# Channel weights loaded by SyncE at the start in fp32, and a table's reordering moved behind two loads, in a sparse-attention and spectral-mixing kernel

## The chip, the cores and the metric

The kernel runs on one core of a Trainium2 chip. The metric is the device time of one execution in microseconds, the median of several runs; lower is better. The profile is one execution recorded by the hardware profiler on that core.

## The reference, cut to what matters

The first half is attention over 8 batches, 8 heads, 576 positions and 64 dimensions a head. Heads 0 to 3 see the last 32 positions ("local"), heads 4 to 7 see every 32nd position ("strided"). The second half takes the result as `x` (8 x 576 x 512), mixes its lowest 64 Fourier modes with two complex weight matrices per mode, and ends with a layer whose matrix is `w_ch`, the channel weights that the change is about.

```python
scores = np.where(masks[None, :, :, :], scale * q @ k.T, -1e9)   # local or strided mask by head
x = softmax(scores) @ v                                          # (8, 576, 512)
X = np.fft.rfft(x, axis=1)
Yr = np.einsum('bmd,mde->bme', Xr, w_r) - np.einsum('bmd,mde->bme', Xi, w_i)
Yi = np.einsum('bmd,mde->bme', Xr, w_i) + np.einsum('bmd,mde->bme', Xi, w_r)
y = np.fft.irfft(Y, n=S, axis=1)
u = x + y
return u + np.maximum(u @ w_ch, 0.0)                             # w_ch is 512 x 512
```

All inputs and the output are fp32 in DRAM. `w_r` and `w_i` are 64 x 512 x 512 each, 134 MB together, and are by far the largest input.

## The kernel before, in words

The kernel computes in f16 with fp32 sums. Loads from DRAM that GpSimd issues convert fp32 to f16 on the way; loads that SyncE (`nc.sync`) or ScalarE (`nc.scalar`) issue copy without converting. Each engine works through its own queue in the order in which the program emits instructions, and the order is written by hand.

The work comes in these stages:

1. **Strided heads**, a loop over 8 batches (L832). `load_str` (L214) brings v, q and k of one or two batches into a ring of 12 slots. `str_front` gives the steps that transpose them; `str_scores` and `str_values` compute attention into `xb`; `dft(b - 1, 1)` transforms the batch before with a table `cFs`. `load_loc` and `w_fetch`, at the head of each turn of the loop, issue later loads on GpSimd: q, k, v of the local heads and the first spectral weights.
2. **Local heads**, a second loop over 8 batches (L863), with `mode_pair` (L589), the spectral product for two modes, between the steps. In this loop's turn 6 stands the load of the channel weights, `w_ch_fetch` (L197).
3. **The other half of the modes**, with `w_turn` (L896), which reorders the channel weights on TensorE, and `premix` (L726), which multiplies x by them.
4. **The last modes and the output**, stored by SyncE (L1071).

The spectral weights are streamed through a ring of five pairs, `wring`. Three more pairs are guests: their place in memory belongs to a tile that is needed only later. The names of these places are in `GUEST = {1: "Y0", 2: "X0", 7: "YT"}` (L148), so pair 7 lies where the spectra tile `YT` comes later. `w_fetch` issues the next pair when a pair of places is free; `mode_pair` calls it after the products that freed one.

The Fourier table `cT` is loaded by SyncE. `strided_tokens` (L330), on GpSimd, clears two margins and writes a reordered copy of `cT` into the tile `PL`. `fourier(1)` (L338) transposes that copy on TensorE into the table `cFs`, which `dft(b, 1)` reads first in batch 1; `fourier(0)` makes the other table after batch 1. At the start GpSimd's queue holds, in this order: the loads of batches 0 and 1 (9 DMAs), `strided_tokens`, the loads of batches 2 and 3 (6 DMAs), and the first spectral weights. `fourier(1)` is emitted after the eighth of batch 0's ten front steps (L829).

Of the kernel before, what the change touches and what calls it, by code (L numbers as in the profile page):

```python
# [10 lines left out]
FP = mybir.dt.float32  # L11
# [7 lines left out]
DM = 512  # L19
# [37 lines left out]
def kernel(  # L57
# [10 lines left out]
    nc = tc.nc  # L68
# [3 lines left out]
    big = ctx.enter_context(tc.tile_pool(name="big", bufs=1))  # L72
# [13 lines left out]
    def psum(kind, half=False, pair=False):  # L86
        if pair:
            return pss[kind].tile([128, 2, 512], FP, tag=kind, name=kind)
        if half:
            return pss[kind].tile([128, 1024], F16, tag=kind, name=kind)  # L90
        return pss[kind].tile([128, 512], FP, tag=kind, name=kind)
# [15 lines left out]
    def const_load(eng, *which):  # L107
        for n in which:
            eng.dma_start(cs[n][:, 0 : hosts[names.index(n)].shape[1]], drams[n])
# [46 lines left out]
    w_chs = {}  # L156
    w_ch = big.tile([128, 4, DM], F16, name="w_ch")
# [3 lines left out]
    def w_fetch(n=1):  # L161
        free_pairs[0] += n
        while len(w_tiles) < 2 * NM:
            i = len(w_tiles)
            pair = i // 2
            nm = 4 if pair in QUADS else 2
            if 2 * free_pairs[0] < nm:
                return
            free_pairs[0] -= nm // 2
            half, m = ORDER[i]  # L170
            if pair in GUEST:
                wt = big.tile([128, 2, 4, DM], F16, tag=GUEST[pair], name="wt")
            else:
                a = 2 * ((pair - sum(g < pair for g in GUEST)) % NWBUF)
                wt = wring[:, a : a + nm]
            single = []
            for ri, src in enumerate((moe_w_r, moe_w_i)):
                dst = wt[ds(64 * ri, 64)].rearrange("p m c e -> p m (c e)")
                rows = src[m : m + nm, ds(256 * half, 256), :].rearrange(
                    "m (p c) e -> p m (c e)", c=4  # L180
                )
                if ri and not m:
                    dst, rows = dst[:, 1:nm], rows[:, 1:nm]
                if i in UNEVEN and not ri:
                    a = 0
                    for n in UNEVEN[i]:
                        nc.gpsimd.dma_start(dst[a : a + n], rows[a : a + n])
                        a += n
                elif i < 2 * NM - 4:
                    nc.gpsimd.dma_start(dst, rows)  # L190
                else:
                    single += [(j, ri, dst[:, j], rows[:, j]) for j in range(nm)]
            for _, _, to, rows in sorted(single, key=lambda x: x[:2]):
                nc.gpsimd.dma_start(to, rows)
            w_tiles.extend(wt[:, j] for j in range(nm))

    def w_ch_fetch():  # L197
        nc.gpsimd.dma_start(w_ch, moe_w_ch.rearrange("(c p) e -> p c e", p=128))
        w_chs["n"] = w_ch

# [11 lines left out]
    def load_str(b, nb):  # L214
        for vi in (2, 0, 1):
            n = 3 * (b % 4) + SLOT[vi]
            two = ring[:, n : n + 4 : 3, :]
            src = SRC[vi][b - b % 2 : b - b % 2 + 2, 4:8].rearrange(
                "b h (c r) d -> (h c) b (r d)", r=32
            )  # L220
            if nb == 2:
                nc.gpsimd.dma_start(two[0:64], src[0:64])
            else:
                nc.gpsimd.dma_start(ring[0:64, n, :], src[0:64, b % 2])
            if b % 2 == 0:
                nc.gpsimd.dma_start(two[64:72], src[64:72])

    def load_loc(*bs):
        for b in bs:
            if b >= B:  # L230
                return
            for vi in (2, 0, 1):
                nc.gpsimd.dma_start(
                    loc_in(b, vi),
                    SRC[vi][b, 0:4].rearrange("h (cb i) d -> (h cb) (i d)", i=18),
                )
# [17 lines left out]
    def act_copy(out, in_):  # L254
        nc.scalar.activation(out=out, in_=in_, func=ACTF.Copy)  # L255
# [74 lines left out]
    def strided_tokens():  # L330
        nc.gpsimd.memset(cs["cT"][:, S:640], 0.0)
        nc.gpsimd.memset(PL[:, S : S + NCB], 0.0)
        nc.gpsimd.tensor_copy(
            out=PL[:, 0:S].rearrange("p (q r c) -> p q r c", q=2, c=NCB),
            in_=cs["cT"][:, 0:S].rearrange("p (c r q) -> p q r c", q=2, r=16),
        )

    def fourier(half):  # L338
        tp = psum("tp", half=True)
        n, nt = (108, 6) if half else (128, 5)  # L340
        for t in range(nt):
            if half:
                lhs = PL[:, ds(288 * (t // 3) + NCB * JG[t % 3][0], 108)]
            else:
                lhs = cs["cT"][:, ds(128 * t, 128)]
            nc.tensor.transpose(tp[0:n, ds(128 * t, 128)], lhs, idn)
        F = cs["cFs"] if half else cs["cFl"]
        src = tp[0:n, 0 : 128 * nt].rearrange("p (t g r m) -> p r t g m", t=nt, g=4, r=2)
        for r in range(2):
            (nc.vector.tensor_copy if r else act_copy)(  # L350
                out=F[0:n, 1 + r].rearrange("p t (g m) -> p t g m", g=4), in_=src[:, r]
            )
        nc.vector.tensor_scalar(
            out=F[0:n, 0], in0=F[0:n, 2], scalar1=-1.0, scalar2=None, op0=AluOp.mult
        )
# [433 lines left out]
    const_load(nc.scalar, "cI", "cM6", "cM5")  # L789
    load_str(1, 1)  # L790
    const_load(nc.sync, "cT", "cMl")
    strided_tokens()
    load_str(2, 2)
    w_fetch()

    def str_front(b):
        return [
            lambda: str_v(b, 0), lambda: str_v(b, 1),
            lambda: str_v(b, 2), lambda: str_q(b, 0),
            lambda: str_back(b, 0),  # L800
            lambda: str_back(b, 1), lambda: str_q(b, 1),
            lambda: str_k(b, 0),
            lambda: str_k(b, 1), lambda: str_k(b, 2),
        ]
# [13 lines left out]
    for i, w in enumerate(first):  # L818
        w()
        if i == 0:  # L820
            nc.vector.memset(vT[:, 1152:1216], 0.0)
            for t in v16:
                nc.vector.memset(t[:, :, 0:2], 1.0)
                nc.vector.memset(t[:, :, 130:132], 1.0)
        if i == 2:
            nc.vector.memset(PS, 0.0)
        if i == 5:
            nc.vector.memset(kzs[1], 0.0)
        if i == 7:  # L829
            fourier(1)  # L830
    SPLIT = [0, 2, 4, 5, 7, 8, 10]
    for b in range(B):  # L832
        if b in (1, 3):
            load_str(b + 3, 2)
        load_loc(*[(), (), (), (), (0,), (1, 2), (3,), (4, 5)][b])
        w_fetch([2, 1, 1, 1, 1, 1, 0, 0][b])
        front = str_front(b + 1) if b + 1 < B else loc_front(0)
        for t in range(6):
            str_scores(b, t)
            if b > 0:  # L840
                if t < 2:
                    str_values(b - 1, 4 + t)
                elif t == 2:
                    dft(b - 1, 1)
            if t >= 2:
                str_values(b, t - 2)
            for w in front[SPLIT[t] : SPLIT[t + 1]]:
                w()
        if b == 1:
            nc.vector.memset(PL[:, 0:PS0], 0.0)  # L850
            fourier(0)
# [11 lines left out]
    for b in range(B):  # L863
        load_loc(b + 6)
        front = loc_front(b + 1) if b else [lambda: None] * 4 + front1[4:]
        scores = [lambda h=h: loc_scores(b, h, False) for h in range(4)]
        ends = [lambda h=h: loc_scores(b, h, True) for h in (0, 2)]
        values = [lambda h=h: loc_values(b, h) for h in range(4)]
        work = [
            scores[0], front[0], scores[1], ends[0], front[1], values[0], front[2],  # L870
            scores[2], front[3], values[1], scores[3], front[4], ends[1], front[5],
            values[2], front[6], values[3], front[7], lambda: dft(b, 0),
        ]
        if b == 6:
            work.insert(0, w_ch_fetch)
        n = 0
        nm = NMODES[b]
        for mi in range(nm):
            upto = -(-len(work) * (mi + 1) // nm)
            for w in work[n:upto]:  # L880
                w()
            n = upto
            mode(0, sum(NMODES[:b]) + mi)
# [12 lines left out]
    def w_turn(half, cp):  # L896
# [14 lines left out]
    work = [  # L911
        lambda half=half, cp=cp: w_turn(half, cp) for half in range(2) for cp in range(2)
    ]
# [76 lines left out]
    for n, i in enumerate([3, 5, 7] + list(range(8, 21))):  # L990
        b, t = n // 2, n % 2 * 2
# [158 lines left out]
```

## Time and profile before

| | us |
|---|---|
| median of 3 runs | 426.48 |
| the three runs | 425.19, 426.83, 426.48 |
| span of the profiled execution, first to last instruction | 423.3 |
| TensorE busy in the span | 336.8 (80%) |
| VectorE, ScalarE, GpSimd busy | 234.9, 218.8, 95.3 |
| packets of GpSimd's DMA queue, share of 16 engines | 96.9% |

The profiled execution's own device time is not recorded apart from its span; the span lies 3.2 us below the median of the runs. In the profile PE is TensorE, DVE VectorE, ACT ScalarE, POOL GpSimd and SP SyncE; `L190` is line 190 of the kernel. The slices cut the span into 40 equal parts and give busy shares in tenths. DMA queue q0 is GpSimd's, q1 SyncE's, q10 ScalarE's. The bytes of a DMA are those that it writes, so an fp32 load that arrives as f16 reads twice as many. A weight load of one pair is two DMAs of 512 KB, one from `w_r` and one from `w_i`; some are four modes long, 1024 KB each.

### The profile page before, as it was taken

How to read it: one execution, taken by the hardware profiler on the slowest of the kernel's cores; microseconds unless marked ns; L12 is line 12 of the kernel's file. 1: busy time of each engine (PE TensorE's matmuls, PEld its weight loads, DVE VectorE, ACT ScalarE, POOL GpSimd, SP SyncE). 2: the span in 40 equal slices, each digit the busy share in tenths (PEclk: the TensorE clock that was granted, in tenths of full speed). 3: DMA queues.
4: the chain of work that ended last, by engine and by line, in shares of the span. 5: the costliest groups of instructions: out<-in, count | busy, mean ns of one | idle time of the engine just before them, and what ended most of it. 6: DMA issues, size and time to landing. Idle time of an engine off the chain costs nothing.

```text
span 423.3 us, 9718 instructions
## 1 busy us (share of the span) xinstructions
PE 336.8 (80%) x4164; PEld 204.2 (48%) x4164; DVE 234.9 (56%) x470; ACT 218.8 (52%) x391; POOL 95.3 (23%) x165
## 2 busy tenths in 40 slices
PE   2977878779999198889874959896778989888994
PEld 2866766654666055556542425453344534445331
DVE  3788878851455034545323325864385547555794
ACT  1687778642656056565753323622162356443772
POOL 7332333322422011102122102212101232210200
PEclk9999999957999689999998789999798999999999
DMA  8999999999999999999999999999999999998598
GB/s 147 213 213 213 214 211 214 210 212 211 214 213 213 215 213 216 213 215 214 212 215 212 213 213 214 214 213 214 213 213 210 210 212 216 212 214 163 198 379 316
DMA packets 30346, 91.62 MB, mean 216 GB/s; under 512 B 3872, under 2 KB 4640, under 8 KB 30304
## 3 DMA queue, kind: packets, MB, share of 16 engines
q0 software_dynamic: 24624, 81.28, 96.9%
q1 hardware_dynamic: 5248, 9.65, 6.2%
q8 instruction: 32, 0.52, 0.5%
q10 hardware_dynamic: 432, 0.08, 0.1%
q14 instruction: 10, 0.08, 0.0%
HBM read 162.83 MB, written 9.44 MB: 407 GB/s over the span
## 4 chain that ended last, share of the span: by engine, by line
PE 38%; DMA 36%; DVE 15%; ACT 5%; issue 3%; POOL 1%; DVEq 0%; POOLq 0%; ACTq 0%
DMA wring<-in_moe_w_i_dram 28%; PE y L601 9%; PE sc L739 5%; DMA ring<-in_q_dram 5%; DMA wring<-in_moe_w_r_dram 4%; DVE xb L245 3%; DVE yy L774 2%; ACT X L255 2%; DVE kz L287 2%; PE p L1010 2%; PE y L536 2%; PE tp L417 2%; PE sc L463 2%; PE sc L536 1%; PE p L1031 1%
## 5 line engine op out<-in xcount | busy, mean ns | idle before, releaser
L601 PE MATMUL y<-wring,X 128*32 128x512 f16 (+1 forms) x424 | 65.0, 418 | 25.8 <-DMA wring<-in_moe_w_i_dram 25.7
L190 POOL DMA_DIRECT2D wring<-in_moe_w_r_dram x39 | 23.5, 604 | 200.1 <-PE y L601 176.8
L601 PEld LDWEIGHTS <-X 128*32 128x32 f16 (+1 forms) x448 | 27.5, 139 | 43.4 <-DMA wring<-in_moe_w_i_dram 26.5
L749 DVE COPY xo<-tp 128x512 f16<-128x512 f16 x32 | 22.1, 692 | 36.9 <-PE tp L747 36.8
L748 ACT ACTIVATE v<-sc 128x512 f16<-128x512 f32 x32 | 19.1, 597 | 45.1 <-PE sc L739 45.1
L255 ACT ACTIVATE yr<-y 128x512 f16<-128x512 f32 x28 | 16.7, 597 | 43.2 <-PE y L601 43.0
L739 PE MATMUL sc<-w_cp,xT 128*128 128x512 f16 x128 | 36.1, 404 | 1.9 <-DVE xT L707 1.9
L245 DVE TENSOR_TENSOR xb<-av,rec 90x256 f16<-90x256 f32 (+2 forms) x80 | 36.0, 450 | 2.8
L493 ACT ACTIVATE PL<-sc 128x480 f16<-128x480 f32 (+1 forms) x48 | 26.9, 578 | 20.2 <-PE sc L479 19.9
L244 DVE RECIPROCAL rec<-av 90x4 f32<-90x4 f32 (+2 forms) x80 | 14.6, 183 | 37.8 <-PE av L508 28.3
L424 DVE COPY qT<-tp 128x576 f16<-128x576 f16 x16 | 11.9, 752 | 39.3 <-PE tp L417 39.3
L190 POOL DMA_DIRECT2D wring<-in_moe_w_i_dram x42 | 25.4, 605 | 9.8 <-DMA wring<-in_moe_w_i_dram 3.8
L984 DVE TENSOR_TENSOR xo<-p,xo 128x1024 f16<-128x1024 f32 x16 | 19.6, 1225 | 13.8 <-PE p L782 13.8
L382 ACT ACTIVATE PL<-sc 90x360 f16<-90x360 f32 (+1 forms) x48 | 22.7, 490 | 6.9 <-PE sc L375 6.4
L255 ACT ACTIVATE v<-p 128x1024 f16<-128x1024 f32 x16 | 16.4, 1023 | 17.1 <-PE p L782 17.1
L255 ACT ACTIVATE v<-tp 128x640 f16<-128x640 f16 (+1 forms) x24 | 19.0, 807 | 11.6 <-PE tp L451 8.8
L417 PE MATMUL tp<-cI_s,ring 64*64 64x64 f16 x864 | 22.8, 198 | 2.1 <-DVE qT L424 1.7
L463 PE MATMUL sc<-cMl_s,cI_s 128*128 128x480 f16 (+1 forms) x48 | 18.9, 393 | 5.2 <-ACT PL L493 3.6
L255 ACT ACTIVATE kz<-tp 64x360 f16<-64x360 f16 (+1 forms) x32 | 18.9, 592 | 6.2 <-PE tp L417 5.2
L280 PE MATMUL tp<-cI_s,ring 72*128 72x72 f16 x256 | 15.4, 207 | 8.4 <-DMA ring<-in_v_dram 6.9
L417 PEld LDWEIGHTS <-ring 64*64 64x64 f16 x864 | 18.0, 112 | 8.3 <-issue 4.2
L1054 ACT ACTIVATE rl<-p 128x1024 f32<-128x1024 f32 (+1 forms) x19 | 18.4, 979 | 4.9 <-PE p L1031 3.0
(146 smaller groups left out, 736.6 us busy)
## 6 DMA issues: line engine op xcount, KB each, us to landing
wring<-in_moe_w_r_dram POOLq DMA_DIRECT2D x17, 1024.0 KB, 13.5
wring<-in_moe_w_i_dram POOLq DMA_DIRECT2D x16, 1024.0 KB, 17.7
wring<-in_moe_w_i_dram POOLq DMA_DIRECT2D x24, 512.0 KB, 15.3
wring<-in_moe_w_r_dram POOLq DMA_DIRECT2D x22, 512.0 KB, 13.4
out_dram<-osb SPq DMA_DIRECT2D x14, 512.0 KB, 3.4
ring<-in_v_dram POOLq DMA_DIRECT2D x8, 288.0 KB, 13.3
ring<-in_q_dram POOLq DMA_DIRECT2D x8, 288.0 KB, 13.6
ring<-in_k_dram POOLq DMA_DIRECT2D x8, 288.0 KB, 13.1
```

The lines of the kernel that those rows point to most:

```text
L190: nc.gpsimd.dma_start(dst, rows)
L245: nc.vector.tensor_tensor(out=dst, in0=val.rearrange("p h (q c) -> p h c q", c=4), in1=rec[0:n, 0:pieces] .to_broadcast((n, pieces, 64)) . ...
L255: nc.scalar.activation(out=out, in_=in_, func=ACTF.Copy)
L382: nc.scalar.activation(out=PS[0:n, ds(POFF[t], 4 * n)], in_=scp[0:n, 0 : 4 * n], func=ACTF.Exp, scale=SCALE,)
L417: nc.tensor.transpose(tp[ds(64 * hp, 64), ds(64 * i, 64)], qn[ds(64 * hp, 64), ds(64 * (9 * g + i), 64)], idn[ds(64 * hp, 64), ds(64 * hp, ...
L463: nc.tensor.matmul(scp[:, 0 : n * times].rearrange("p (h x) -> p h x", h=times), idn, mask_rows("cMl", n, times), start=True, stop=False,)
L493: nc.scalar.activation(out=dst, in_=src, func=ACTF.Exp, scale=SCALE)
L601: nc.tensor.matmul(yp[ds(a, 32), :], Xh[half][pr, c].rearrange("p b r (h m) -> p (b r h) m", h=2)[:, :, mm % 32], wt[pr, XC[c], :], start= ...
L739: nc.tensor.matmul(vp, xT[:, ch], w_chs["cp"][:, ch, :], start=(ch == 0), stop=(ch == 3),)
L748: nc.scalar.activation(out=v0, in_=vp, func=ACTF.Copy)
L749: nc.vector.tensor_copy(out=xo.rearrange("p (h q c) -> p h q c", h=2, c=4), in_=tp[:, 0:512].rearrange("p (h c q) -> p h q c", h=2, c=4),)
L984: nc.vector.tensor_tensor(out=xo, in0=up[:, 0:n], in1=xo, op=AluOp.add)
```

## The change

The load of the channel weights moves from GpSimd's queue (turn 6 of the second loop) to SyncE's queue, behind the constants at the beginning. Since SyncE's loads do not convert, the weights arrive as fp32 in a tile of their own, `w_f`, that takes the place of `YT` and so of the guest weight pair 7. ScalarE then rounds a quarter of it to f16 into `w_ch` at the end of each of the batches 1 to 4 of the strided loop. On GpSimd, the loads of batches 2 and 3 go ahead of `strided_tokens`. `fourier(1)` moves from inside batch 0's front steps to the end of batch 0's turn.

```diff
-    def w_ch_fetch():
-        nc.gpsimd.dma_start(w_ch, moe_w_ch.rearrange("(c p) e -> p c e", p=128))
+    def w_ch_load():
+        w_chs["f"] = big.tile([128, 4, DM], FP, tag="YT", name="w_f")
+        nc.sync.dma_start(w_chs["f"], moe_w_ch.rearrange("(c p) e -> p c e", p=128))
         w_chs["n"] = w_ch
+
+    def w_ch_round(c):
+        act_copy(w_ch[:, c], w_chs["f"][:, c])
...
     const_load(nc.sync, "cT", "cMl")
+    w_ch_load()
+    load_str(2, 2)
     strided_tokens()
-    load_str(2, 2)
     w_fetch()
...
-        if i == 7:
-            fourier(1)
...
+        if b == 0:
+            fourier(1)
+        if 1 <= b <= 4:
+            w_ch_round(b - 1)
         if b == 1:
             nc.vector.memset(PL[:, 0:PS0], 0.0)
             fourier(0)
...
-        if b == 6:
-            work.insert(0, w_ch_fetch)
```

## The prediction

> **What bounds the kernel now.** I read the page's slices first, then the table of DMA queues.
>
> ```profile
> PE   2977878779999198889874959896778989888994
> DMA  8999999999999999999999999999999999998598
> GB/s 147 213 213 213 214 211 214 210 212 211 214 213 213 215 213 216 213 215 214 212 215 212 213 213 214 214 213 214 213 213 210 210 212 216 212 214 163 198 379 316
> q0 software_dynamic: 24624, 81.28, 96.9%
> ```
>
> From the second slice to about 389 us the DMA engines move 210 to 216 GB/s without a pause, nearly all of it in one queue: GpSimd's, which reads fp32 and writes f16. 81.28 MB at 212 GB/s are 383.4 us; with a start at about 3 us and the 1.5 us lost early (below) that makes 388 us, against the 390.6 us at which the last load is seen to land. TensorE has holes in the same slices. The chain of waits, in order of time, says who waits for whom:
>
> ```profile
> 110.63 15.19 DMA wring<-in_moe_w_r_dram
> 126.10 21.10 DMA wring<-in_moe_w_i_dram
> ...
> 346.62 14.75 DMA wring<-in_moe_w_i_dram
> 361.65 19.09 DMA wring<-in_moe_w_i_dram
> 381.03 9.58 DMA wring<-in_moe_w_i_dram
> 391.46 1.05 PE y L758 x4
> ```
>
> TensorE waits for weights again and again, and the last weights land at 390.61; what follows (32.7 us to the end of the span, 423.3) hangs on that landing. So the time is the stream's start, plus its bytes at 212 GB/s, plus what it loses where it runs below that, plus a fixed tail. An instruction on TensorE, ScalarE or GpSimd counts only if it starves the stream. The only place where it is visibly below rate is the beginning; the table of stretches shows that (columns: stretch, length, busy time of the five engines, TensorE clock, DMA share, GB/s):
>
> ```profile
> 1.50:3.00 1.50, 0.00 (x0) 0.00 (x0) 0.64 (x1) 0.90 (x1) 1.50 (x3) 1.00 0.81 183
> 3.00:4.50 1.50, 0.00 (x0) 0.00 (x0) 0.00 (x0) 0.38 (x1) 1.50 (x4) 1.00 0.90 120
> 4.50:6.00 1.50, 0.00 (x0) 0.00 (x0) 0.00 (x0) 0.00 (x0) 1.25 (x3) 1.00 1.08 176
> 6.00:7.50 1.50, 0.62 (x11) 0.65 (x12) 0.06 (x1) 0.00 (x0) 0.87 (x4) 1.00 1.06 161
> 7.50:9.00 1.50, 0.50 (x9) 0.32 (x6) 1.31 (x7) 0.83 (x2) 1.50 (x3) 1.00 1.00 191
> 9.00:10.50 1.50, 1.43 (x18) 1.46 (x19) 1.20 (x3) 0.00 (x0) 1.29 (x3) 1.00 1.05 199
> ...
> 207.00:214.00 7.00, 5.19 (x60) 3.27 (x57) 1.03 (x4) 4.31 (x9) 0.00 (x0) 1.00 1.12 210
> ```
>
> Against 213 GB/s the five stretches from 3.0 to 10.5 us lack 93, 37, 52, 22 and 14 GB/s, times 1.5 us: 327 KB, or 1.53 us of the stream. That is all the room that the beginning has. The last line is where the channel weights pass now: still 210 GB/s.
>
> **Part by part.** *The load taken out of GpSimd's queue.* 128 x 4 x 512 in f16 are 0.524 MB, and in 207:214 the stream kept its rate: 0.524 / 213 = 2.46 us. All that follows in the queue can come 2.46 us earlier. The issue itself (0.80 us on GpSimd at 197.28) lies before 7.46 us in which GpSimd waits for TensorE: nothing.
>
> *The load put on SyncE's queue.* It now writes fp32, 1.049 MB. No row shows an fp32 load, so I bound it. The stream reads two bytes for each one that it writes, 2 x 213 = 426 GB/s: 2.46 us. The fp32 output at the end (400:410) moves 380 GB/s: 2.76 us. I take 2.6: rows of 2 KB as in the output, but read from DRAM as in the stream. SyncE has the two constant loads ahead of it (0.74 to 1.56 us) and nothing behind it until the outputs at 394.96, so it is issued at about 1.6 and moves data from about 2.5 us, together with GpSimd's first loads. If the engines are full this takes 2.6 us away from GpSimd's queue, and the whole is +0.1. What it moves in the holes is free: at most the 1.53 us; at least the clear hole of 3.0:4.5, where the DMA share is 0.90 and 93 x 1.5 = 140 KB, 0.65 us, are missing. I take 1.2, nearer to the upper end, because GpSimd, not the engines, sets the early rate: it had issued eight DMAs when it had to sit 0.88 us for the first to land (below).
>
> The Trainium skill, page DMA: Bandwidth & Descriptors, section Issuing engines are not separate DMA queues, speaks against this change: DMAs from different issuing engines run on the same 16 engines and interleave, and only the issuing time is saved. By it the sum of the two loads is 2.46 out and 2.46 in, no change. The trace agrees with it wherever the engines are full, as in 207:214; the first 10 us are where they are not.
>
> *Loads of batches 2 and 3 ahead of the table's reordering.* GpSimd's timeline:
>
> ```profile
> 6.63 0.51 POOL L224 DMA_DIRECT2D ring<-in_k_dram  x1 [0.88 <-DMA ring<-in_v_dram]
> ...
> 7.26 1.17 POOL L333 COPY PL<-cT_s 128x576 f16<-128x576 f16 x1
> 8.37 0.59 POOL L222 DMA_DIRECT2D ring<-in_v_dram  x1
> ...
> 12.99 0.58 POOL L190 DMA_DIRECT2D wring<-in_moe_w_r_dram  x1 [0.70 <-DMA ring<-in_q_dram]
> ```
>
> The two memsets and the copy (7.13 to 8.43) leave the front of the six load issues and stand before the first weight issue. The first of the six can go 1.2 us earlier; the next ones wait for landings anyway, so the gain is between 0 and the 22 and 14 GB/s missing after 7.5 us (54 KB, 0.25 us), and that is already counted as room. The weights' first issue now stands behind 1.3 us of reordering, of which its own 0.70 us wait hides half. Seven DMAs (1.9 MB, 9 us) are in flight then, so the stream does not run dry; without that cover the cost would be 0.6 us. I take 0.
>
> *The table's transposes behind batch 0.* The same instructions, later: 6 transposes (0.80 us of TensorE), one ScalarE copy (0.49), two VectorE steps (0.36 + 0.26). Their first reader is the transform at 24.14, in batch 1. Batch 0 has 0.8 us less ahead of it. Nothing.
>
> *Four roundings on ScalarE.* The nearest row is the 128x512 fp32 to f16 copy at 597 ns, from PSUM: 4 x 0.60 = 2.4 us at the ends of batches 1 to 4 (about 31 to 60 us). Queued behind each are the next batch's exponentials, for which TensorE waits. So TensorE is up to 2.4 us later at 60 us, and up to 2.6 more because the first loads share the engines. It is covered: in 140:160 TensorE is busy 12.06 of 20 us, waiting for weights, and GpSimd's loads land 13 us after their issue, so the queue is that deep when its issues wait for TensorE (23.62, 26.52, 30.50). Uncovered it would be up to 5 us. The fp32 copy lies in the buffer of weight pair 7, whose load waits for the fourth rounding: about 60 us plus lateness, against an issue at 75.33. Nothing.
>
> **The sum.** -2.46 + 2.6 - 1.2 = -1.1 us; by the bounds from -1.5 (2.46 in, 1.53 in holes) to -0.35 (2.76 in, 0.65 in holes), and +0.3 with no hole. On the profiled execution: span 423.3 to 422.2. The median of the runs, 426.48, is 3.2 above this span; I carry that over: 425.4.
>
> **Rivals.** *Paid in full:* the holes are not idle engines but slow ones (the share reads 1.06 and 1.08 in 4.5:7.5, which speaks for it; the 0.90 before speaks against). Then -2.46 + 2.6 = +0.1: 426.6. This is also where the rule of the Trainium skill quoted above (DMA: Bandwidth & Descriptors) would put it.
>
> *Wholly hidden:* the channel weights fill 2.46 us of real idle time, with the head of the load before 3.0 us (share 0.81) counted in and the earlier issue filling the rest: 424.0. For it speaks that GpSimd's issue sets the early pace; against it, that only 1.53 us are missing from 3.0 on. A gain of more than 0.5% (2.13 us) needs this.
>
> *Turns cost more than bytes:* SyncE's rows alternate with GpSimd's packets on each engine, and each turn stalls the other queue. The trace has small packets of ScalarE's queue among GpSimd's, the last mask's, landing 5.4 us after issue where its twin took 2.5. If the whole loss of 1.53 us came from these masks (2 x 128 rows, 16 for each engine), a turn would cost 0.096 us, and 32 turns (512 rows of 2 KB over 16 engines) 3.1 us: -2.46 + 2.6 + 3.1 = +3.2, 429.7. It brings over 0.5% from 0.062 us a turn on. Against it: those masks have landed by about 7 us, and the loss goes on to 10.5.
>
> **How the numbers follow.** About 0.5%, 2.13 us, is what a measurement of this kernel can tell from no change (its three runs lie 1.64 us apart). Partly hidden, my forecast: 0.5. Paid in full: 0.18. Wholly hidden: 0.17. Turns, slower: 0.15. The first two fall within 0.5%, but runs scatter and the forecast's lower end is near the border, so I move 0.03 from them to faster: 0.20, 0.65 and 0.15. The range runs from wholly hidden, 424.0, past the paid-in-full case with its dearer end (2.76 in: 426.8) and a first part of the third rival (0.02 us a turn, 0.64 us): 427.4. Outside lie most of that rival and runs below 424.0, together about 0.2.
>
> **What would show it.** Right: SyncE's queue carries about 1.05 MB more and GpSimd's 0.52 less; the stretches from 3.0 to 10.5 move more bytes in all while GpSimd's queue alone moves fewer; the last weights land at about 389.5; the tail keeps its 32.7 us; the late stream keeps its 212 GB/s. Wrong: a landing at 390.6 or later (paid in full, or turns, and then the first 16 us show less than 213 GB/s of f16 with no hole filled), a landing at 388.2 (wholly hidden), or an unchanged landing shift with a longer tail. A new wait of GpSimd for ScalarE before pair 7, or a rate below 210 after 20 us, would mean that the cover I named was not there.

## The result and the profile after

The changed kernel takes 429.69 us (median of 429.53, 429.60, 429.77 and 433.08); the kernel before, in the same rounds, 425.94. The medians lie 3.75 us, or 0.9%, apart. The ratio worked out from all runs, in which 433.08 weighs too, is 1.0108, with a 95% interval of 1.0070 to 1.0146. So the change is slower by about 1%, where 425.4 was forecast. The profiled execution took 429.53 us, its span is 427.8, against 423.3 before. In the changed kernel's page the slices of TensorE, of the DMA engines and of the bytes moved, and the lines of GpSimd's queue (q0) and SyncE's (q1), are these:

```profile
PE   1787888868999379888966859896687987888994
...
DMA  8999999999999999999999999999999999998598
GB/s 177 204 213 212 212 214 211 212 211 211 214 212 213 214 214 214 215 213 213 205 198 210 214 215 214 214 206 209 207 212 195 211 214 214 214 212 168 188 380 317
...
q0 software_dynamic: 24096, 80.75, 95.9%
q1 hardware_dynamic: 5776, 10.70, 7.2%
```

GpSimd's queue carries 0.53 MB less, SyncE's 1.05 MB more, as the change says. Two things are new in the row of bytes. First, the beginning. The first two slices moved (177 + 204) x 10.70 us = 4.07 MB, against (147 + 213) x 10.58 = 3.81 MB before. That is only 0.26 MB more, although the new load brought 1.049 MB; so 0.78 MB of the f16 stream was pushed back, 0.784 / 213 = 3.7 us; and the two slices are together 0.2 us longer than before's, which makes 3.9 us. Second, from the 19th to the 36th slice, where before never fell under 210, there are now 205, 198, 206, 209, 207 and 195. Counted against 214 GB/s, these 18 slices lack 3.75 us of the stream; before they lacked 0.89.

The table of stretches of the changed kernel shows the beginning (columns as in the prediction):

```profile
1.50:3.00 1.50, 0.00 (x0) 0.00 (x0) 0.64 (x1) 0.89 (x1) 1.50 (x3) 1.00 0.99 196
3.00:4.50 1.50, 0.00 (x0) 0.00 (x0) 0.00 (x0) 0.39 (x1) 1.50 (x4) 1.00 0.81 89
4.50:6.00 1.50, 0.00 (x0) 0.00 (x0) 0.00 (x0) 0.00 (x0) 1.25 (x3) 1.00 0.95 229
6.00:7.50 1.50, 0.00 (x0) 0.00 (x0) 0.00 (x0) 0.00 (x0) 0.00 (x0) 1.00 1.03 244
7.50:9.00 1.50, 0.11 (x3) 0.14 (x4) 0.00 (x0) 0.00 (x0) 0.51 (x1) 1.00 1.07 250
```

The clear hole of 3.0:4.5, which the load was to fill, got deeper: 89 GB/s instead of 120, and SyncE's queue moved only 0.02 MB in it. From 4.5 on more bytes are moved than before (229 to 250 GB/s), but fp32 bytes do not stand for f16 ones: the DMA share reads 0.95 to 1.07, as before, so the engines were as busy as ever.

GpSimd's timeline of the changed kernel shows who felt it:

```profile
7.71 0.51 POOL L228 DMA_DIRECT2D ring<-in_k_dram  x1 [1.96 <-DMA ring<-in_v_dram]
9.04 0.59 POOL L226 DMA_DIRECT2D ring<-in_v_dram  x1 [0.82 <-DMA ring<-in_v_dram]
11.52 0.57 POOL L230 DMA_DIRECT2D ring<-in_v_dram  x1 [1.88 <-DMA ring<-in_q_dram]
...
18.35 0.58 POOL L190 DMA_DIRECT2D wring<-in_moe_w_r_dram  x1
```

GpSimd waits for the landing of its earlier loads before it issues the next (1.96 us instead of 0.88 at the ninth), and the first weight load is issued at 18.35 instead of 12.99. Last, the chain of waits, in order of time, at the places where before was shown, and around them:

```profile
3.03 9.55 DMA ring<-in_q_dram
...
116.21 14.37 DMA wring<-in_moe_w_r_dram
130.87 21.09 DMA wring<-in_moe_w_i_dram
...
220.93 14.71 DMA wring<-in_moe_w_i_dram
...
385.54 9.58 DMA wring<-in_moe_w_i_dram
395.97 1.05 PE y L762 x4
```

In the chain of before, the first of these waits and the one after 216 us were:

```profile
3.04 5.90 DMA ring<-in_q_dram
...
216.06 16.93 DMA wring<-in_moe_w_i_dram
```

The wait for q ends at 12.58 instead of 8.94 (+3.6). The wait of 130.87 ends at 151.96; its twin of before (126.10 + 21.10) at 147.20: +4.75. The next one ends at 235.64, +2.6 against 233.00, and the last weights land at 395.12 instead of 390.61: +4.5. From that landing to the end of the span there are 32.7 us, exactly as before.

So the account by the slices is: +3.9 at the start, +0.3 in the 3rd to 18th slice, -2.46 because the channel weights' 0.524 MB are out of GpSimd's queue, +2.9 in the later slices; sum +4.6, seen +4.5. (That is more than the 3.75 us between the medians: before's profiled execution, with a span of 423.3, lies 0.7 below the median span of 424.0 of the same kernel in the later rounds.) Two terms are to be explained: why the start cost 3.9 us and not the 1.4 of the prediction (2.6 less 1.2), and why 2.9 us were lost 200 us later, which the prediction did not have at all.

### The profile page after: what moved, and what is told of

It reads as the page before. It is cut to its first block, busy times and chain, and to the rows that moved or that the text cites. A ratio compares the mean times of both kernels' runs of the same rounds, so it can differ in the third digit from the quotient of the medians.

```text
span 427.8 us, 9728 instructions
## 1 busy us (share of the span) xinstructions
PE 339.4 (79%) x4164; PEld 207.0 (48%) x4164; DVE 235.1 (55%) x470; ACT 221.0 (52%) x395; POOL 94.5 (22%) x164
## 3 DMA queue, kind: packets, MB, share of 16 engines
q1 hardware_dynamic: 5776, 10.70, 7.2%
## 4 chain that ended last, share of the span: by engine, by line
PE 38%; DMA 34%; DVE 15%; ACT 7%; issue 4%; POOL 1%; DVEq 0%; POOLq 0%; ACTq 0%
DMA wring<-in_moe_w_i_dram 28%; PE y L605 9%; PE sc L743 5%; DMA wring<-in_moe_w_r_dram 3%; ACT X L259 3%; DVE xb L249 3%; DVE yy L778 2%; DMA ring<-in_q_dram 2%; PE sc L540 2%; DVE kz L291 2%; PE y L540 2%; PE tp L421 2%; PE sc L467 2%; DVE osb L1073 1%; PE p L1015 1%
## 5 line engine op out<-in xcount | busy, mean ns | idle before, releaser
L259 ACT ACTIVATE v<-p 128x1024 f16<-128x1024 f32 x16 | 16.4, 1024 | 17.2 <-PE p L786 17.2
```

## The experiments

Medians and intervals are against the kernel before in the same rounds. The landing is that of the last weights in the profiled execution, 390.61 in the kernel before and 395.12 in the changed one. The first five runs take the change apart.

**Without any load of the channel weights** (the kernel before, `w_ch` set to a constant).

```diff
-        nc.gpsimd.dma_start(w_ch, moe_w_ch.rearrange("(c p) e -> p c e", p=128))
+        nc.gpsimd.memset(w_ch, 0.03)
```

> The kernel before without the load of the channel weights: a GpSimd memset of the same tile stands in its place (the channel weights are a constant). This is what the removal alone is worth. Theory S, the stream sets the time everywhere: 2.46 us less, about 423.5, and the last weights land at 388.2. Theory L, after about 200 us the loop 'TensorE frees a place, GpSimd issues, the load lands' sets the time and the channel weights only filled what the stream had to spare: less than 1.2 us gained, 424.8 to 426, with stretches below 205 GB/s between 205 and 230 us.

Measured: 423.72 us, ratio 0.9952 (0.9933 to 0.9970). The chain of waits of this run, at its end:

```profile
126.51 21.09 DMA wring<-in_moe_w_i_dram
...
216.39 14.50 DMA wring<-in_moe_w_i_dram
...
378.92 9.62 DMA wring<-in_moe_w_i_dram
```

The wait near 147 us ends 0.4 us later than before's (147.60), the next 2.1 us earlier than before's 233.00, and the last landing is 388.54, -2.1. Taking 2.46 us of bytes out of GpSimd's queue is worth 2.1 us, all of it after the place where they were. The load in its new place therefore costs 3.75 + 2.1 = 5.9 us of the medians.

**The early load alone** (the changed kernel with the old order of `strided_tokens`, `load_str(2, 2)` and `fourier(1)`).

```diff
-    load_str(2, 2)
     strided_tokens()
+    load_str(2, 2)
...
+        if i == 7:
+            fourier(1)
...
-        if b == 0:
-            fourier(1)
```

> The channel weights early by SyncE and the four roundings, but the loads of batches 2 and 3, the reordering and the table's transposes where they were before. If the early load alone makes the loss: 429 to 430, with GpSimd's queue 3.5 to 4.2 us late after its first 3 MB. If the new order takes part (GpSimd's first weight issue stood 1.3 us behind the reordering and came at 18.35 instead of 12.99): 427 to 428.5.

Measured: 428.73 us, 1.0063 (1.0039 to 1.0087). Its profiled execution, 433.96, was the slowest of its seven, so only the median is read. It lies between the two ranges: 2.9 of the 3.75 us, with overlapping intervals.

**The order alone** (the kernel before with the new order).

```diff
-    strided_tokens()
     load_str(2, 2)
+    strided_tokens()
...
-        if i == 7:
-            fourier(1)
...
+        if b == 0:
+            fourier(1)
```

> The new order alone: loads of batches 2 and 3 ahead of the reordering, the table's transposes after batch 0, the channel weights loaded by GpSimd in turn 6 as before. If the order costs nothing, as predicted: 425.4 to 426.4. If it costs through the first weight issue: up to 0.6 us more. If the earlier issue fills the early hole: up to 0.3 us less.

Measured: 425.58 us, 0.9990 (0.9973 to 1.0006): nothing that can be told from no change. Its first weight load is issued at 13.40, so the 18.35 of the changed kernel is not the order's doing. With the run above: the loss, or nearly all of it, belongs to the load.

**The changed kernel without the roundings** (`w_ch` set to a constant; the load stays).

```diff
-        if 1 <= b <= 4:
-            w_ch_round(b - 1)
+        if b == 1:
+            nc.gpsimd.memset(w_ch, 0.03)
```

> The changed kernel without ScalarE's four roundings; the fp32 load runs and nobody reads it, and a GpSimd memset after batch 1 fills the f16 channel weights with a constant. If the roundings are hidden, as predicted: 429 to 430, unchanged within noise. If they make TensorE late enough to starve the stream: 427.5 to 428.5.

Measured: 429.62 us, 1.0104 (1.0052 to 1.0157), the same as with them, though four runs from 428.23 to 433.38 tell it no finer than about 2 us. Within that the four roundings (629 to 631 ns each) are hidden.

**Half of the load** (256 of the 512 rows, each read by two roundings).

```diff
-        nc.sync.dma_start(w_chs["f"], moe_w_ch.rearrange("(c p) e -> p c e", p=128))
+        nc.sync.dma_start(
+            w_chs["f"][:, 0:2], moe_w_ch[0:256].rearrange("(c p) e -> p c e", p=128)
+        )
...
-        act_copy(w_ch[:, c], w_chs["f"][:, c])
+        act_copy(w_ch[:, c], w_chs["f"][:, c % 2])
```

> The changed kernel with only the first 256 rows of the channel weights loaded, 0.52 MB, and used twice; four roundings as before. If the early lag goes with the bytes: 1.9 to 2.1 us instead of 3.9, and about 427. If a fixed disturbance of the first loads makes most of it: 2.8 us or more, and 428 or above.

Measured: 427.68 us, 1.0043 (1.0013 to 1.0072). GpSimd's loads between 40 and 140 us land 1.4 to 2.4 us later than before's (one 0.8), about half of the 4.75 of the whole load. So the lag at the start goes with the bytes. The time does not decide between the two theories: the median lies between their forecasts, and the profiled execution, 425.78, is among the fastest of the ten.

The next five ask what the start's 3.9 to 4.75 us are made of. A load counts as landed when the last of the 16 DMA engines has done its part; the trace also tells when the first had. Both lags, against the kernel before, are given for the weights landing between 50 and 60 us. They scatter: in five profiled executions without an early load they are -0.2 to 0.5 us on the first engine and 0.1 to 0.45 on the last, and in four others with the load as in the changed kernel 3.4 to 3.9 and 4.5 to 5.5.

**The same load at 25 us, with GpSimd's queue full.**

```diff
+        nc.vector.memset(w_chs["f"][:, :, 0:1], 0.0)
...
-    w_ch_load()
...
-        if 1 <= b <= 4:
-            w_ch_round(b - 1)
+        if b == 0:
+            w_ch_load()
+        if 3 <= b <= 4:
+            w_ch_round(2 * b - 6)
+            w_ch_round(2 * b - 5)
```

> The changed kernel, but SyncE's load waits until VectorE has cleared one column of the fp32 tile at the end of batch 0, at about 25 us, when GpSimd's queue is full; two roundings each stand at the ends of batches 3 and 4. Bytes, rows and queue are the same. If the loss is made by sharing the engines at the start: only the bytes are paid, the stream is late by 2.4 to 2.7 us after the load instead of 3.9, the slowest engine no more than the others, and the time is 425.5 to 426.8. If mixing an fp32 load into the stream costs beyond its bytes wherever it is: late by 3.7 or more, 428 to 430.

Measured: 428.39 us, 1.0048 (1.0028 to 1.0068). The lag is 2.9 us on the first engine and 3.9 on the last; in the changed kernel 3.9 and 4.75. So there was no free room at the start, rather the contrary: the same load makes the stream 0.5 to 1 us later there than in a full stream. And the time falls into the second theory's range: at 25 us, too, the load costs more than its bytes.

The packets of the two queues show where this goes (the profile's lines for DMA queues, for one stretch of time; columns: packets, MB, and the time of the packets as a share of the 16 engines' time; packets can overlap, so a share can exceed 100%). From 3 to 18 us GpSimd's queue in before, then GpSimd's and SyncE's in the changed kernel; last, SyncE's in this run from 24 to 45 us:

```profile
q0 software_dynamic: 933, 2.83, 102.4%
...
q0 software_dynamic: 687, 2.03, 74.9%
q1 hardware_dynamic: 528, 1.05, 29.5%
...
q1 hardware_dynamic: 528, 1.05, 14.8%
```

SyncE's packets occupy the engines for 29.5% of 15 us, 4.4 us, at the start, and for 14.8% of 21 us, 3.1 us, in the full stream (in the late run below 14.7% of 179 to 200 us, again 3.1). GpSimd's share at the start falls by 27.5 points of 15 us, 4.1 us. That is the lag, within its scatter: SyncE's load costs the time that its packets hold the engines, more than its bytes at the stream's rate (2.46).

**An f16 load early, in GpSimd's queue** (after `strided_tokens`, no roundings).

```diff
-    w_ch_load()
...
     strided_tokens()
+    nc.gpsimd.dma_start(w_ch, moe_w_ch.rearrange("(c p) e -> p c e", p=128))
+    w_chs["n"] = w_ch
```

> The changed order, but the channel weights come as f16 through GpSimd's queue, ahead of the first spectral weights (issue at about 14 us), with no fp32 tile and no rounding. If only the start's sharing is at fault: -2.46 late and +2.46 early, 425.5 to 426.5. If being early is at fault in itself (TensorE then frees places as late as before and the loads after 210 us wait for it): 427 to 428.5.

Measured: 427.46 us, 1.0034 (1.0011 to 1.0057). The lag is 2.4 us on the first engine, what the bytes say, and 3.5 on the last. The time lies in the second range. Even with no second queue and no fp32 an early load shows dearer than it was at 197 us, where it made 2.1.

**Rows of 8 KB, and of 1 KB,** instead of 2 KB (with 8 KB rows the weights come in another order of their rows).

```diff
-        nc.sync.dma_start(w_chs["f"], moe_w_ch.rearrange("(c p) e -> p c e", p=128))
+        nc.sync.dma_start(w_chs["f"], moe_w_ch.rearrange("(p c) e -> p c e", p=128))
```

> The changed kernel, but the channel weights come as 128 rows of 8 KB instead of 512 rows of 2 KB (a partition gets four neighbouring rows of the matrix, so the weights are in another order). Bytes, place and order are the same; SyncE's turns on each engine fall from 32 to 8. Theory T, each turn costs beyond its bytes: the early lag of 3.9 us falls to 2.8 to 3.1 and the time to about 428.6. Theory E, the first loads land late because 1 MB shares the engines with them, and GpSimd, with eight DMAs in flight at most, cannot refill the stream: the lag stays at 3.5 us or more and the time at 429 or above, since the same bytes pass even earlier.

```diff
-        nc.sync.dma_start(w_chs["f"], moe_w_ch.rearrange("(c p) e -> p c e", p=128))
+        for e in (0, 256):
+            nc.sync.dma_start(
+                w_chs["f"][:, :, e : e + 256],
+                moe_w_ch[:, e : e + 256].rearrange("(c p) e -> p c e", p=128),
+            )
```

> The changed kernel with SyncE's load in two DMAs of half rows: 1024 rows of 1 KB instead of 512 of 2 KB, the same bytes. If a part of the loss goes with the number of rows (8 KB rows gave 428.8 instead of 429.7): the stream is late by 4.5 us or more after its first 3 MB instead of 3.9, and the time is 430.5 or more. If not: 429 to 430.

Measured: 428.80 us, 1.0059 (1.0029 to 1.0089), with 8 KB; 430.67, 1.0123 (1.0083 to 1.0163), with 1 KB. The middle, 429.69, is the changed kernel. The order is the one that turns between the queues would give, but the steps are 0.9 and 1.0 us and the intervals overlap. At 0.096 us a turn, 32 more turns on each engine would have cost 3.1 and 24 fewer given back 2.3. The lags are 3.3 us on the first engine and 4.2 on the last with 8 KB, 3.9 and 5.5 with 1 KB (whose profiled execution, 432.96, was the slowest of its four). SyncE's packets hold the engines for 3.6 us with 8 KB (23.9% of 3 to 18 us) and 5.1 with 1 KB (23.4% of 3 to 25 us), where 2 KB took 4.4. By these single executions a turn costs an estimated 0.02 to 0.03 us, a third of the rival's price at most. Turns are a part, not the cause.

**The load late on SyncE's queue** (at 180 us, the roundings in turns 6 and 7 of the second loop).

```diff
+        nc.vector.memset(w_chs["f"][:, :, 0:1], 0.0)
...
-    w_ch_load()
...
-        if 1 <= b <= 4:
-            w_ch_round(b - 1)
...
+        if b == 5:
+            w_ch_load()
+        if b > 5:
+            work.append(lambda b=b: w_ch_round(2 * b - 12))
+            work.append(lambda b=b: w_ch_round(2 * b - 11))
```

> The changed kernel, but SyncE's fp32 load waits for a VectorE memset in turn 5 of the second loop (about 185 us, near the place that GpSimd's load had), and the roundings stand at the ends of turns 6 and 7. Bytes, rows and queue as in the change. If mixing SyncE's rows into the stream is the loss: 427.5 to 429, like the load at 25 us (428.4). If being early is the loss: 425.5 to 426.8, near the kernel before.

Measured: 426.36 us, 1.0010 (0.9993 to 1.0027), no change. The row of bytes of this run's page, and its last landing in the chain of waits:

```profile
GB/s 151 210 213 214 212 212 213 210 211 212 213 214 213 213 214 212 215 237 231 214 215 212 214 213 214 213 212 215 211 214 211 213 214 215 213 213 158 196 379 318
```

```profile
126.25 21.31 DMA wring<-in_moe_w_i_dram
...
381.10 9.56 DMA wring<-in_moe_w_i_dram
```

The same fp32 load shows as 237 and 231 in the 18th and 19th slice, and weights there land 2.8 us later (GpSimd's load issued at 179.4). But TensorE does not wait for the stream between 147 and 216 us: in the chain of waits of before no DMA stands between those two. GpSimd's issues stay within 0.4 us of before's until about 200 us, and the last landing is 390.66, +0.05. So fp32 through SyncE does not itself cost 4 us. At this place, where TensorE does not wait for the stream, it costs no more than GpSimd's f16 load did, as far as the interval tells (-0.3 to 1.1 us); ahead of the wait that ends at 147 us it costs more.

Then the later loss. First the splits: the weight loads of three pairs are cut into uneven parts (`UNEVEN`), fitted by hand to the order of before.

```diff
-    UNEVEN = {64: (25, 12, 27), 84: (6, 54, 4), 94: (10, 54)}
+    UNEVEN = {}
```

> The changed kernel without the uneven splits of three weight loads (positions 64, 84 and 94 of the order, 64 rows each in two or three pieces). After the channel weights' old place the slowest engine's landings lie 2.5 us behind the kernel before and at the end 4.5; two of the steps between stand at these three loads. If the splits, made for the old lead of some DMA engines, cause them: against its partner below the gap shrinks to 2 to 2.8 us (from 3.75). If not, the gap stays at 3.3 us or more.

> The kernel before without the three uneven splits: the partner of the run above. If the splits even out a lead that the kernel before has: 1 to 2.5 us slower than before, 427 to 428.3. If they do nothing there: 425.4 to 426.2.

Measured: the changed kernel without them 428.80 us, 1.0063 (1.0039 to 1.0088); the kernel before without them 425.96, 1.0007 (0.9997 to 1.0017). The gap is 2.84 instead of 3.75 us, between the two forecasts: they may carry 0.9 of it, with overlapping intervals. The place of the loss is another one here. The changed kernel without the splits lacks only 0.10 us in the slices from the 19th to the 36th, but its 11th slice falls to 185 GB/s. There GpSimd waits 5.41 us for TensorE before the load that it issues at 108.40 (in before 1.20, issued at 99.33). The run with the early f16 load shows the same: 0.90 us in the later slices, 184 GB/s in the 11th.

Then TensorE itself. Both kernels with three quarters of the spectral products and of `premix`'s products left out, all loads kept:

```diff
-        steps = [(c, mm) for c in range(4) for mm in (m, m + 1)]
+        steps = [(0, mm) for mm in (m, m + 1)]
...
-            for c in range(4):
+            for c in range(1):
...
-        for ch in range(4):
+        for ch in range(1):
```

> The kernel before with three quarters of the spectral products (only c = 0 of the four chunks) and of premix's products left out, so that part of the computation is not done; all loads stay. TensorE then has room everywhere after 100 us. It is the base for the run below. Theory A (the last 2 us of the loss come because a late TensorE issues late and the stream runs dry) and theory B (the stream itself moves less, whoever issues) expect the same here: the stream alone sets the time, the last weights land within about 3 us of the 390.6 us of before, and the slices from 200 us on lose no more than before's 0.9 us against 214 GB/s; time 415 to 428 us.

> The changed kernel with the same three quarters of the spectral and premix products left out. Early lag of the stream as in the changed kernel, 3.7 us by bytes and about 1 us more on the slowest engine; the channel weights are no longer in the late stream, -2.46. Theory A: with room on TensorE the issues catch up, the stream keeps 212 to 214 GB/s after 200 us, and the last landing and the time are 1.2 us (by bytes) to 2.3 us (slowest engine) above the lightened before. Theory B: the loss does not hang on TensorE, and the difference stays 3.5 us or more.

Measured: before so lightened 425.30 us, 0.9989 (0.9970 to 1.0008); the changed kernel so lightened 427.74, 1.0039 (1.0021 to 1.0058). Row of bytes of the lightened changed kernel's page, and a line of its chain of waits:

```profile
GB/s 176 206 210 212 213 212 212 212 213 210 213 214 212 215 214 214 214 214 215 214 214 214 212 215 214 214 213 213 215 213 213 214 215 212 215 212 154 194 379 318
```

```profile
182.45 19.50 DMA wring<-in_moe_w_i_dram
```

TensorE now waits for the stream at 182 us, where before it did not: it has room. The start is as slow as in the changed kernel (176, 206), and the loads up to 217 us land 4.6 us later than before's. But the later slices now hold 212 to 215: they lack 0.25 us, where the changed kernel lacked 3.75 and the lightened before 1.04. When the channel weights' place in the stream is passed, the lag falls from 4.6 to about 2 and stays there or below; the last landing is 391.85, only 1.2 above before's and 0.65 above the lightened before's 391.20. The medians say 2.44 where it was 3.75: just above the 1.2 to 2.3 of theory A (a late TensorE), below the 3.5 or more of theory B. The profiled execution, 426.07, is the fastest of its nine (median 427.74), so its landing gap of 0.65 is likely too small. A TensorE with room thus takes away a part of the later loss, as theory A has it: TensorE frees places late, and the stream runs dry. How large that part is stays unsettled.

No run points to a version that beats both kernels: what beats before leaves the load out, and the others are equal or slower.

## Why the prediction was wrong, step by step

**Right.** The changed order, the transposes and the roundings cost nothing that can be measured. The fixed tail is 32.7 us to the tenth. Pair 7's place brought no wait into the chain: GpSimd waits 2.13 us before its load; the profile puts this down to a copy on ScalarE, but in before the wait was 2.04, and the last rounding had ended 16 us earlier, at 64.1. 2.46 us of bytes at 197 us are worth 2.1 us. And the prediction said beforehand what would show it wrong: "a landing at 390.6 or later (paid in full, or turns, and then the first 16 us show less than 213 GB/s of f16 with no hole filled)". That is what came, and so did the sign that the cover was not there, "a rate below 210 after 20 us" (205, 198, 195 in the later slices).

**The step that failed first:** "What it moves in the holes is free ... I take 1.2", on top of 2.6 for the bytes. Fill was nil, and the load's price 3.9 us by the bytes of two slices. The 2.6 was too small as well: it came from bytes, where SyncE's packets held the engines for 3.1 us in a full stream and 4.4 us at the start. The reason was in the table of stretches of before: from 4.5 us on the DMA share stood at 1.00 to 1.08 while only 161 to 199 GB/s were moved. Engines that are busy and slow were no room; from 3 to 18 us GpSimd's packets alone took 102.4% of their time, so it was not GpSimd's issuing, as the prediction had it, that set the pace. The rival "paid in full" named those shares; I gave it 0.18. Of the 4.75 us by which the slowest engine fell behind, the runs with other places for the load put 2.4 down to bytes (f16, GpSimd's queue), 1.1 to the slowest of 16 engines falling behind the first (3.5 against 2.4), 0.4 to fp32 in a second queue (3.9 at 25 us), and about 0.9 to the start (4.75). Each is one execution against one, and the 0.4 is no larger than the scatter.

**The step that failed second:** "It is covered: in 140:160 TensorE is busy 12.06 of 20 us, waiting for weights, and GpSimd's loads land 13 us after their issue ..." For the roundings that held, as far as the run without them tells; for the load it did not. TensorE's wait there is no cover for a late stream; it is the place where the stream's lateness becomes TensorE's. The wait of 126.10 ends 4.75 us later, one for one, and then TensorE sets the pace until 216 us and hands the lateness to GpSimd's issues, which are 4.9 us late at 216 us (220.93 for 216.06). There the queue has to live from its depth, while the load that went out has just brought the landings forward by 2.4 us. The stretches of the changed kernel at that place, and the one of before that covers 220:225:

```profile
210.00:215.00 5.00, 3.35 (x38) 1.95 (x33) 0.69 (x2) 2.99 (x8) 1.25 (x2) 1.00 1.00 188
...
220.00:225.00 5.00, 3.23 (x45) 2.14 (x47) 1.28 (x4) 1.23 (x3) 1.26 (x2) 1.00 0.99 186
...
285.00:290.00 5.00, 4.95 (x44) 2.86 (x44) 2.95 (x7) 1.28 (x3) 0.52 (x1) 1.00 1.14 192
...
320.00:325.00 5.00, 3.25 (x28) 1.77 (x26) 4.29 (x8) 2.58 (x5) 1.22 (x2) 0.92 1.00 182
```

```profile
220.00:225.00 5.00, 4.01 (x40) 1.97 (x34) 0.00 (x0) 3.39 (x9) 2.48 (x4) 1.00 1.06 214
```

The DMA share, 1.00 and 0.99 against 1.06, shows little of it; the landings show more. The load issued at 201.47 is done on its first engine at 212.48, the next, issued at 210.76, at 218.50: 6.0 us apart, where loads of this size (1024 KB) stand 4.9 apart in the full stream. So the engines that were first stood idle there for an estimated 1.1 us.

So "All that follows in the queue can come 2.46 us earlier" held at its place and was given back within 110 us: the landing lag against before goes 4.9, 2.3 (load issued at 210.76), 3.2 (near 260 us), 4.0 (near 300 us), 5.2 (near 335 us), 4.5 (end). The prediction treated the sum as one of bytes from start to end; in this execution bytes ahead of the 147 us wait were paid twice, once there and again as late issues.

**The rivals.** "Turns cost more than bytes" has the right side and even the right number, 429.7, but the runs with other row sizes do not bear its price: the number is luck. "Paid in full" has the right mechanism for the start and stops there: it had nothing for the later loss. By the rule of the Trainium skill that I weighed (DMA: Bandwidth & Descriptors, Issuing engines are not separate DMA queues) the bytes should have cancelled. The late load on SyncE's queue agrees with it, 426.36 against 425.72; the early one does not cancel, because the place is different, not the bytes. (In before's 207:214, to which the prediction pointed, SyncE's queue moves nothing, so that stretch could not test the rule.)

**The offset.** I carried 3.2 us from span to median. In the runs since, an execution takes 1.7 to 1.9 us more than its span (one takes 3.4), so 1.4 of these 3.2 were the scatter of three runs. That made the forecast higher, nearer to the result, for no good reason.

**Open.** Why the slowest engine loses 1 us more than the first with any early load, and why the same packets hold the engines 1.3 us longer at the start than in a full stream. How the later loss divides between uneven splits (0.9 by medians) and TensorE's lateness as such. The later loss also differs from execution to execution: from about 225 us to the end the landing lag grows by 1.9 us in the changed kernel, 3.2 without the roundings, 2.0 with the load at 25 us, 0.5 with the early f16 load and 0.4 without the splits; and by 1.4 in the order-alone run, which has no early load (its execution, 427.17, was the slowest of ten). No run held TensorE's granted clock fixed, which was 0.942 in before's profiled execution and 0.935 in the changed kernel's. So the direction of the later loss is better shown than its size.

## What to carry to other kernels

Where loads and TensorE bound the time by turns, price a moved load by the time that its packets hold the DMA engines (here 3.1 us in a full stream and 4.4 at the start, 2.5 by bytes), and at the next wait that hangs on the stream: ahead of such a wait every microsecond is passed on to TensorE and may return as late issues, while in a stretch that TensorE bounds the same bytes cost almost nothing extra. A low GB/s with a DMA share near 1 need not be room to fill: here nothing was filled. Lateness that the profile shows as "covered by a wait" must be followed to the end of that wait: ask what is issued after it.

## What the runs showed of the hardware

A 1.049 MB fp32 load beside GpSimd's converting stream took 15.4 us from issue to landing at the start, 17.2 at 25 us and 17.3 at 180 us. The Trainium skill says that each DMA engine takes turns between the queues of the two kinds (DMA: Bandwidth & Descriptors, SWDGE vs HWDGE vs iDMA); the trace fits this. From 3 to 18 us both queues' packets pass, with 74.9% and 29.5% of the engines' time, and the last engine of GpSimd's first six loads is done 1.8 to 3.0 us after the first, where it was 0.9 to 1.3 in before.

The 16 engines drift apart: the same load's first and last engine finish 1 to 2 us apart up to 80 us, 4 us near 200 and up to 7 near 290 in the kernel before (9 in the changed one), and 2 us again at the end. What is waited for is the last one, and an early load delayed it by about 1 us more than the first (4.75 against 3.9, 3.5 against 2.4).

With less work on TensorE its granted clock was lower: the kernel before shows a mean granted clock of 0.942, the same kernel with three quarters of the products left out 0.848. It had room all the same; its time is the stream's.
